# Seventeen products of zeros on TensorE, in the front of a windowed attention with two MoE layers

## The chip, the cores and the metric

The kernel runs on one core of a Trainium2 chip. The metric is the time of one execution on the device in microseconds (us). Before the change three runs took 639.21, 640.41 and 640.44 us; the median is 640.41 us.

## What is computed

Windowed attention with block summaries, then two feed-forward layers on its output, all in float32:

```python
# q, k, v: (2, 8, 768, 64); block 32, window 16, scale 1/8
k_sum = k in blocks of 32, max over the block        # 24 summary keys
v_sum = v in blocks of 32, mean over the block
scores_l = scale * q @ k.T, only where |pos_q - pos_k| < 16
scores_s = scale * q @ k_sum.T + log(32)
a = softmax over [scores_l, scores_s]
x = a @ [v, v_sum]                                   # (1536, 512)
h = relu(x @ w_in);  x = (h * h) @ w_out             # d_ff 2048
xn = x / sqrt(mean(x * x) + 1e-6) * rms_g
out = (silu(xn @ w_gate) * (xn @ w_val)) @ w_out2    # d_ff 1536
```

## The kernel before, in words

The 1536 tokens are 12 groups of 128 (two batches of 6 groups). For a group g the attention has these steps, each a helper of the program:

- `qprep(g)` transposes the queries of groups g and g+1 on TensorE (`qps`, L431) and scales them on ScalarE into `qT` (L433).
- `scores(g)` multiplies queries and keys into two PSUM tiles `s0_g` and `s1_g`. For the first four groups the mask is added by products of an identity with the mask, one ahead (L486) and one behind (L501) the score products (L493).
- `softmax(g)` takes maxima on VectorE (`mx`, L529), exponentials with sums on ScalarE (`t`, `sm`, L535), and normalises on VectorE (L543 to L545). For g < 3 it works in two halves of the heads.
- `ptrans(g)` transposes the probabilities on TensorE (`pps`, L555) and copies them to `pT` on ScalarE (L558).
- `av(g)` multiplies them with the values (`xps1_g`, L578); `split_xs` puts the result into a high part `xhi` on ScalarE (L568) and a low part `xlo` on VectorE (L569).

All weights come as float32 words and are turned into pairs of a high and a low part by a chain of ScalarE steps (L203, L204, L223) and VectorE steps (L210, L211, L214, L217, L224), one chunk at a time: `wi0` to `wi3` and `wo0` to `wo3` in the front. A product of two split matrices is three products of parts (`mm3`). The first feed-forward layer's first chunks (`h_pair`, L617; `y_pair`, L639) are interleaved with the attention of the later groups, so that `h0_0_0` (hidden chunks 0 and 1 of token groups 0 and 1) follows soon after attention group 1. A hidden chunk is squared and split in turn (`r`, L798 and L799; `hhi`, `hlo`, L628 and L629). The rest of the program is products of the two feed-forward layers.

What sets the order: the program text gives the order in which steps are recorded, and a scheduler with a model of the engines lays the instructions out on each engine's own queue; `after(mark)` (`tc.issue_after`) makes it place what is recorded inside it behind the marked instruction. PSUM tiles come from pools with tags: in the front the tags "a" and "x" turn by turn (two banks each), and "h" with two banks.

At the start of the program, TensorE multiplies a tile of zeros `wz` with itself ten times (`WARM`) into a PSUM tile `ws`, and nothing reads the result:

```python
    for _ in range(WARM):
        nc.tensor.matmul(ws, wz, wz, start=True, stop=True)
```

Of the kernel before, what the change touches and what calls it, by code (L numbers as in the profile page):

```python
# [10 lines left out]
F32 = mybir.dt.float32  # L11
# [21 lines left out]
def tile_window_attention_moe_moe2(  # L33
# [13 lines left out]
    nc = tc.nc  # L47
    B, H, S, D = q.shape
    NT, DM = out.shape
    P = 128  # L50
# [38 lines left out]
    psB = ctx.enter_context(tc.tile_pool(name="psB", bufs=1, space=PSUM))  # L89
# [208 lines left out]
    WARM = 10  # L298
# [30 lines left out]
    mark = {}  # L329

    def after(*marks):
        es = ExitStack()
        for m in marks:
            es.enter_context(tc.issue_after(mark[m].ins))
        return es
# [3 lines left out]
    def psA(name, shape=None):  # L339
        tag = rot["tags"][rot["i"] % len(rot["tags"])]  # L340
        rot["i"] += 1
        pool, bufs = {"a": (psB, 2), "h": (psB, 2), "y": (psY, MT // 2), "x": (psX, 2)}[tag]
        return pool.tile(shape or [P, 512], F32, tag=tag, name=name, bufs=bufs)
# [20 lines left out]
    def prep_begin(b):  # L364
        ksum = ap_.tile([P, NPAIR, NB], F32, tag="ksum", name=f"ksum{b}", bufs=1)
        state[b] = ksum
# [54 lines left out]
    def qload(g):  # L421
        b, r = divmod(g, GPB)
        state[("q", g)] = token_chunk(q, b, r // 2, f"qr{g}")

    def qprep(g):
        qr = state.pop(("q", g))
        qT2 = ap_.tile([P, NPAIR, 2 * P], F32, tag="qT", name=f"qT{g}", bufs=QB)
        for j in range(2):
            ps = psA(f"qps{g}_{j}", [P, NPAIR, P])
            for p in range(NPAIR):  # L430
                nc.tensor.transpose(ps[:, p, :], qr[:, j, p * P : (p + 1) * P], ident)  # L431
            with after(*((("exp", 1),) if g == 2 else ())):
                nc.scalar.mul(qT2[:, :, j * P : (j + 1) * P], ps, scale)  # L433
        state[("qT", g)] = state[("qT", g + 1)] = qT2
# [28 lines left out]
    def vload(g, eng=None):  # L463
        b, r = divmod(g, GPB)
        i0 = 2 * g % NVX

        for u in range(2):
            t0 = r * P + u * QT
            rows = [
                (0, G0, t0 - WIN) if t0 else (WIN, WIN, 0),  # L470
                (K1, QT, t0 + WIN) if t0 + QT < S else (K1, QT - WIN, t0 + WIN),
            ]
            for j, n, o in rows:
                (eng or nc.sync).dma_start(
                    vx[j : j + n, i0 + u], v[b, :, o : o + n, :].rearrange("h s d -> s h d")
                )

    def scores(g):
        b, r = divmod(g, GPB)
        qT = state[("qT", g)][:, :, (r % 2) * P : (r % 2 + 1) * P]  # L480
        sl = [psA(f"s{e}_{g}", [P, NPAIR, NK]) for e in range(2)]
        wide = [P, NPAIR, NK]
        if g < NPE:
            for s_ in sl:
                mh = mhi["mid" if r else "first"]
                nc.tensor.matmul(s_, identr, mh.unsqueeze(1).to_broadcast(wide), start=True, stop=False)  # L486
        for p in range(NPAIR):
            for x in range(2):
                for e in range(2):
                    u = (e + x) % 2  # L490
                    o = STEP * (2 * r + u)
                    rr = slice(QT * e, QT * e + QT)
                    mark[("s", g)] = nc.tensor.matmul(  # L493
                        sl[e][QT * u : QT * u + QT, p, :],
                        qT[rr, p, QT * u : QT * u + QT],
                        kT[rr, p, o : o + NK],
                        start=g >= NPE, stop=g >= NPE,
                    )
        if g < NPE:
            for s_ in sl:  # L500
                mark[("s", g)] = nc.tensor.matmul(  # L501
                    s_, identr, mlo.unsqueeze(1).to_broadcast(wide), start=False, stop=True
                )
        state[("s", g)] = sl
# [56 lines left out]
    def split_xs(ps, g, ph):  # L561
        c, m = divmod(g, MT)
        if (ph, c) not in xs:
            new_xs(c, ph)
        hi, lo = xs[(ph, c)]
        pv = ps.rearrange("d (k s) -> d k s", k=KD)
        hv = hi[:, :, m * P : (m + 1) * P]
        mark[("xhi", g, ph)] = nc.scalar.copy(hv, pv)  # L568
        mark[("xlo", g, ph)] = nc.vector.tensor_tensor(lo[:, :, m * P : (m + 1) * P], pv, hv.bitcast(F32), op=ALU.subtract)  # L569

    def av(g):
        pT = state.pop(("pT", g))
        ps = psA(f"xps1_{g}")
        for u in range(2):
            for p in range(NPAIR):
                o = p * P + QT * u
                for e in range(2):
                    nc.tensor.matmul(  # L578
                        ps[QT * e : QT * e + QT, o : o + QT],
                        vx[:, (2 * g + u) % NVX, 2 * p + e, :],  # L580
                        pT[:, e * NPAIR + p, QT * u : QT * u + QT],
                        start=True, stop=True,
                    )
        split_xs(ps, g, 1)
        state["done"] = g
# [131 lines left out]
    def group(g):  # L717

        scores(g)
        if g > 3:  # L720
            vload(g)
        softmax(g)
        if g + 2 < NG and g % 2 == 0:
            qload(g + 2)
# [3 lines left out]
    wz = cpool.tile([P, P], F32, name="wz")  # L728
    nc.vector.memset(wz, 0.0)
    nc.scalar.activation(ss[:, 0:1], wz[:, 0:1], AF.Exp)  # L730
    ws = psY.tile([P, P], F32, tag="y", name="ws", bufs=MT // 2)
    for _ in range(WARM):
        nc.tensor.matmul(ws, wz, wz, start=True, stop=True)
    prep_begin(0)
    for c in range(NC2):
        prep_load(0, c)
# [30 lines left out]
    ptrans(1)  # L767
    qprep(2)
    av(0)
    group(2)  # L770
    vload(2)
    rot["tags"] = ("y",)
    group(3)
    rot["tags"] = ("a", "x")
    av(1)
    vload(3)
    ptrans(2)
# [18 lines left out]
    def square(ps, nm):  # L796
        t = t2(f"r{nm}")
        nc.scalar.activation(t, ps, AF.Relu)  # L798
        nc.vector.tensor_tensor(t, ps, t, op=ALU.mult)  # L799
        return t  # L800
# [36 lines left out]
    for k_ in range(NK2):  # L837
        g, last = 2 * k_ + 3, 2 * k_ + 3 >= NG
        h_pair(k_, 0)
        if k_ == 0:  # L840
            av(2)
            group(4)
# [70 lines left out]
    for i in range(n1 + 2):  # L913
        if i < n1:
# [7 lines left out]
            t = square(ps, f"{c}_{f}")  # L922
# [236 lines left out]
```

## Time and profile before

| | before |
|---|---|
| median of three runs | 640.41 us |
| time of the profiled execution | 640.82 us |
| its span, first to last instruction | 639.1 us |
| TensorE busy | 626.1 us |
| VectorE busy | 457.4 us |
| ScalarE busy | 366.2 us |
| mean granted TensorE clock | 0.987 |

The profile page is one execution as the hardware profiler saw it. PE is TensorE, DVE is VectorE, ACT is ScalarE, SP is the queue that issues most loads. "Busy" of PE is the union of its instructions, which overlap in the pipeline. The granted clock is the share of full speed that TensorE was given: 1.00 is 2.4 GHz and 0.50 is 1.2 GHz. Times within a profile count from the first instruction. A product of two float32 tiles appears as two records on PE, a transpose as one.

### The profile page before, as it was taken

To read this page: it belongs to the slowest core of one execution; us is meant where nothing else is said; L and a number is where in the kernel's file an instruction comes from. 1 tells how busy PE (TensorE), PEld (TensorE's weight loads), DVE (VectorE), ACT (ScalarE), POOL (GpSimd) and SP (SyncE) were. 2 spreads that over 40 slices of the span, in tenths; PEclk is the share of its full clock that TensorE was granted. 3 is DMA by queue.
4 is the path that set the end of the run, shared out by engine and by line. 5 is a ranking of instruction groups with operands and counts; after the bars stand their busy time and mean duration, and the time that the engine had idled before them with its cause. 6 is when DMAs were issued, how large, how long until landed. Compare 5 with 4: busy or idle time off the path is not lost.

```text
span 639.1 us, 9547 instructions
## 1 busy us (share of the span) xinstructions
PE 626.1 (98%) x3578; PEld 518.3 (81%) x3578; DVE 457.4 (72%) x830; ACT 366.2 (57%) x767; POOL 58.1 (9%) x87
## 2 busy tenths in 40 slices
PE   8889999999999999999999999999999999999997
PEld 6568887888888888888888888888888888888885
DVE  4789766969995289986486889489499399561423
ACT  5687676677673266564553767457367277353241
POOL 5021210000000000000000000003004003022040
PEclk9859999999999999999999999999999999999999
DMA  9999812445232123321020115218428319017063
GB/s 255 309 194 159 193 42 50 114 150 179 84 102 96 34 66 100 99 67 34 0 73 28 34 49 182 67 39 179 112 67 172 94 63 183 15 16 118 1 97 101
DMA packets 84430, 64.19 MB, mean 100 GB/s; under 512 B 50368, under 2 KB 73920, under 8 KB 84384
## 3 DMA queue, kind: packets, MB, share of 16 engines
q1 hardware_dynamic: 72976, 51.32, 27.0%
q0 software_dynamic: 11408, 12.26, 13.5%
q8 instruction: 28, 0.46, 0.3%
q14 instruction: 18, 0.15, 0.1%
HBM read 49.94 MB, written 13.63 MB: 99 GB/s over the span
## 4 chain that ended last, share of the span: by engine, by line
PE 87%; DVE 6%; SPq 3%; ACT 2%; DMA 1%; issue 1%; ACTq 0%; DVEq 0%
PE h L617 19%; PE y L639 19%; PE z L639 15%; PE qa L974 10%; PE v L617 5%; PE g L617 5%; PE qc L974 5%; PE qb L974 3%; PE xps L578 2%; SPq L358 2%; PE s L493 1%; PE pps L555 1%; PE xps L595 1%; ACT t L535 1%; DMA raw_wi<-in_moe_w_in_dram 1%; DVE t L521 1%
## 5 line engine op out<-in xcount | busy, mean ns | idle before, releaser
L617 PE MATMUL h<-xhi,w_wi 128*128 128x512 f32 (+1 forms) x480 | 133.5, 352 | 0.0
L639 PE MATMUL y<-w_wo,hhi 128*128 128x512 f32 x384 | 116.7, 392 | 0.4 <-ACT hhi L628 0.4
L617 PEld LDWEIGHTS h<-xhi,w_wi 128*128 128x128 f32 x480 | 86.1, 192 | 12.0 <-ACT t L535 0.2
L639 PE MATMUL z<-w_wp,hhiz 128*128 128x512 f32 x288 | 85.8, 390 | 0.0
L617 PE MATMUL h<-xlo,w_wi 128*128 128x512 f32 (+1 forms) x240 | 84.0, 351 | 0.0
L639 PEld LDWEIGHTS y<-w_wo,hhi 128*128 128x128 f32 x384 | 71.3, 188 | 15.5 <-ACT hhi L628 0.6
L1009 POOL DMA_DIRECT2D out_dram<-zs x40 | 34.9, 1130 | 497.5 <-ACT zs L1005 495.0
L639 PE MATMUL y<-w_wo,hlo 128*128 128x512 f32 x192 | 72.3, 392 | 0.0
L639 PEld LDWEIGHTS z<-w_wp,hhiz 128*128 128x128 f32 x288 | 53.9, 188 | 11.1
L639 PE MATMUL z<-w_wp,hloz 128*128 128x512 f32 x144 | 53.0, 389 | 0.0
L798 ACT ACTIVATE r<-h 128x512 f32<-128x512 f32 x48 | 28.7, 598 | 40.2 <-PE h L617 40.2
L617 PEld LDWEIGHTS h<-xlo,w_wi 128*128 128x128 f32 x240 | 46.1, 192 | 5.9 <-DVE xlo L569 0.2
L799 DVE TENSOR_TENSOR r<-h,r 128x512 f32<-128x512 f32 x48 | 32.9, 685 | 21.5 <-ACT r L798 21.2
L639 PEld LDWEIGHTS y<-w_wo,hlo 128*128 128x128 f32 x192 | 35.7, 188 | 7.3 <-issue 0.2
L628 ACT CAST hhi<-r 128x512 fp32r<-128x512 f32 x48 | 29.7, 620 | 19.2 <-DVE r L799 18.9
L629 DVE TENSOR_TENSOR hlo<-r,hhi 128x512 fp32r<-128x512 f32 x48 | 32.8, 684 | 8.1 <-ACT hhi L628 7.8
L617 PE MATMUL g<-x,w_wg 128*128 128x512 f32 x144 | 34.6, 389 | 0.0
L617 PE MATMUL v<-x,w_wv 128*128 128x512 f32 x144 | 34.6, 389 | 0.0
L1059 DVE TENSOR_TENSOR v<-qc,v 128x512 f32<-128x512 f32 x12 | 8.3, 692 | 35.4 <-ACT v L1058 35.4
L1005 ACT COPY zs<-z 128x512 f32<-128x512 f32 x48 | 26.8, 592 | 11.9 <-PE z L639 11.0
L639 PEld LDWEIGHTS z<-w_wp,hloz 128*128 128x128 f32 x144 | 27.0, 188 | 5.7
L617 PEld LDWEIGHTS g<-x,w_wg 128*128 128x128 f32 x144 | 27.0, 188 | 5.6
(206 smaller groups left out, 1228.3 us busy)
## 6 DMA issues: line engine op xcount, KB each, us to landing
out_dram<-zs POOLq DMA_DIRECT2D x40, 256.0 KB, 6.2
raw_wi<-in_moe_w_in_dram SPq DMA_DIRECT2D x16, 512.0 KB, 5.0
raw_wo<-in_moe_w_out_dram SPq DMA_DIRECT2D x16, 512.0 KB, 4.5
raw_wg<-in_moe_w_gate_dram SPq DMA_DIRECT2D x12, 512.0 KB, 3.4
raw_wv<-in_moe_w_val_dram SPq DMA_DIRECT2D x12, 512.0 KB, 3.6
raw_wp<-in_moe_w_out_dram SPq DMA_DIRECT2D x12, 512.0 KB, 5.8
kr<-in_k_dram SPq DMA_DIRECT2D x12, 256.0 KB, 4.0
qr<-in_q_dram SPq DMA_DIRECT2D x12, 256.0 KB, 5.3
```

Of the source, the lines that this page charges most:

```text
L358: nc.sync.dma_start(t[:, j].rearrange("p (h d) -> p h d", h=H), src[b, :, o : o + P, :].rearrange("h p d -> p h d"),)
L578: nc.tensor.matmul(ps[QT * e : QT * e + QT, o : o + QT], vx[:, (2 * g + u) % NVX, 2 * p + e, :], pT[:, e * NPAIR + p, QT * u : QT * u + QT ...
L617: pe["last"] = nc.tensor.matmul(ps, a_, b_, start=(i == 0), stop=(i == tot - 1))
L628: nc.scalar.copy(hi[:, 0:n], s[:, 0:n]),
L629: nc.vector.tensor_tensor(lo[:, 0:n], s[:, 0:n], hi[:, 0:n].bitcast(F32), op=ALU.subtract),
L639: pe["last"] = nc.tensor.matmul(y, a_[:, ms], b_, start=(first and i == 0), stop=(last and i == 2))
L798: nc.scalar.activation(t, ps, AF.Relu)
L799: nc.vector.tensor_tensor(t, ps, t, op=ALU.mult)
L974: last = nc.tensor.matmul(ps, w[a_][:, kk], x[b_][:, kk], start=start and n == 0, stop=n == 3 * K2 - 1, skip_group_check=not start,)
L1005: nc.scalar.copy(s, ys.pop(m))
L1009: nc.gpsimd.dma_start(out[g * P : (g + 1) * P, :], s, accum_op=ALU.add)
L1059: nc.vector.tensor_tensor(v1[f], C[f], v1[f], op=ALU.add)
```

## The change

Ten lines of the front. The helper `turn_over` records n products of zeros behind the given marks. It replaces the loop at the start (the same ten products), and is called twice more: seven products behind the last product of `av(0)`, ahead of `scores(2)`, and ten behind the last mask product of `scores(3)`. Both write a new PSUM tile `ws2` of the tag "h", which nothing reads. `av` now leaves a mark on its products.

```diff
@@ av(g)
-                    nc.tensor.matmul(
+                    mark[("av", g)] = nc.tensor.matmul(
...
     ws = psY.tile([P, P], F32, tag="y", name="ws", bufs=MT // 2)
-    for _ in range(WARM):
-        nc.tensor.matmul(ws, wz, wz, start=True, stop=True)
+    def turn_over(t, n, *marks):
+        with after(*marks):
+            for _ in range(n):
+                nc.tensor.matmul(t, wz, wz, start=True, stop=True)
+
+    turn_over(ws, WARM)
...
     av(0)
+    ws = psB.tile([P, P], F32, tag="h", name="ws2", bufs=2)
+    turn_over(ws, 7, ("av", 0))
     group(2)
     vload(2)
     rot["tags"] = ("y",)
     group(3)
+    turn_over(ws, 10, ("s", 3))
     rot["tags"] = ("a", "x")
     av(1)
```

The scheduler also lays out other instructions in another order, from group 2 on. Three places show what the prediction speaks of.

TensorE behind scores 3, from the last mask product to the stream of h0_0_0. In the names `pps2_1` is the second half of the transposes of group 2, `xps1_2` the attention output of group 2. Before:

```order
L501 MATMUL s1_3_456<-mstage_84 128x480
L555 MATMUL pps2_0_517<-ident_78,t2_429 120x128 x4
L431 MATMUL qps4_0_530<-ident_78,qr4_448 128x128 x4
L578 MATMUL xps1_1_493<-pT1_360,vx_93 64x64 x8
L555 MATMUL pps2_1_523<-ident_78,t2_429 120x128 x4
L578 MATMUL xps1_1_493<-pT1_360,vx_93 64x64 x8
L578 MATMUL xps1_2_608<-pT2_516,vx_93 64x64
L493 MATMUL s1_4_628<-kT_92,qT4_529 64x120 x8
L431 MATMUL qps4_1_536<-ident_78,qr4_448 128x128 x4
L578 MATMUL xps1_2_608<-pT2_516,vx_93 64x64 x4
L617 MATMUL h0_0_0_542<-xhi1_0_403,w_wi0_555 128x256
L578 MATMUL xps1_2_608<-pT2_516,vx_93 64x64 x2
```

With the change:

```order
L735 MATMUL ws2_407<-wz_98 128x128 x10
L555 MATMUL pps2_0_535<-ident_78,t2_437 120x128 x4
L431 MATMUL qps4_0_548<-ident_78,qr4_456 128x128 x4
L578 MATMUL xps1_1_511<-pT1_360,vx_93 64x64 x8
L555 MATMUL pps2_1_541<-ident_78,t2_437 120x128 x4
L578 MATMUL xps1_1_511<-pT1_360,vx_93 64x64 x8
L431 MATMUL qps4_1_554<-ident_78,qr4_456 128x128 x4
L578 MATMUL xps1_2_626<-pT2_534,vx_93 64x64 x8
L493 MATMUL s1_4_646<-kT_92,qT4_547 64x120 x5
L617 MATMUL h0_0_0_560<-xhi1_0_403,w_wi0_573 128x256
L493 MATMUL s1_4_646<-kT_92,qT4_547 64x120 x3
L617 MATMUL h0_0_2_700<-xhi1_0_403,w_wi2_701 128x256
```

The ten products of zeros stand between scores 3 and the transposes of group 2. Behind the last row four more products of xps1_2 follow, so that ahead of the stream of h0_0_0 there are now 12 of them instead of 7, and one of h0_0_2.

VectorE at the softmax of group 2, beside the conversion of weight chunk wi2 (`x_wi2`). Before:

```order
L211 TENSOR_SCALAR x_wi2_562<-x_wi2_562 128x512
L529 TENSOR_REDUCE mx2_430<-s0_2_407 128x4
L214 SCALAR_TENSOR_TENSOR x_wi2_562<-raw_wi2_347,x_wi2_562 128x512
L529 TENSOR_REDUCE mx2_430<-s1_2_408 128x4
L217 ISA x_wi2_562<-x_wi2_562,u_wi2_563 128x1024
L543 TENSOR_SCALAR sm2_431<-sm2_431 128x4
L529 TENSOR_REDUCE mx3_478<-s0_3_455 128x4
L544 RECIPROCAL sm2_431<-sm2_431 128x4
L529 TENSOR_REDUCE mx3_478<-s1_3_456 128x4
L545 TENSOR_TENSOR t2_429<-t2_429,sm2_431 128x480
```

With the change:

```order
L211 TENSOR_SCALAR x_wi2_580<-x_wi2_580 128x512
L214 SCALAR_TENSOR_TENSOR x_wi2_580<-raw_wi2_347,x_wi2_580 128x512
L217 ISA x_wi2_580<-x_wi2_580,u_wi2_581 128x1024
L529 TENSOR_REDUCE mx2_438<-s0_2_415 128x4
L529 TENSOR_REDUCE mx2_438<-s1_2_416 128x4
L224 TENSOR_TENSOR w_wi2_701<-x_wi2_580,w_wi2_701 128x512
L543 TENSOR_SCALAR sm2_439<-sm2_439 128x4
L544 RECIPROCAL sm2_439<-sm2_439 128x4
L529 TENSOR_REDUCE mx3_486<-s0_3_463 128x4
L545 TENSOR_TENSOR t2_437<-t2_437,sm2_439 128x480
```

The merge (L214) and the add (L217) of wi2 moved ahead of both maxima of group 2, and one maximum of group 3 moved behind the first normalisation. On ScalarE the rounding copy of wi2 (L223) moved from behind the exponentials of group 2 to ahead of them.

ScalarE at the cast of `hhi0_1_0`, behind the last product of y0_0 (its copy is `yp1`), with the change:

```order
L652 COPY yp1_945<-y0_0_1_824 128x512
L805 ACTIVATE r0_1_0_1007<-h0_1_0_982 128x512
L393 COPY kT_92<-kps1_1_1_910 128x2x4x16
L394 COPY kT_92<-kps1_1_1_910 128x2x4x48
L393 COPY kT_92<-kps1_2_0_927 128x2x4x16
L394 COPY kT_92<-kps1_2_0_927 128x2x4x48
L568 CAST xhi1_1_965<-xps1_4_948 128x4x128
L393 COPY kT_92<-kps1_2_1_935 128x2x4x16
L394 COPY kT_92<-kps1_2_1_935 128x2x4x48
L433 ACTIVATE qT6_969<-qps6_0_970 128x4x128
L628 CAST hhi0_1_0_1010<-r0_1_0_1007 128x512
```

Before, the cast stood ahead of all copies of keys (`kT`) of batch 1, three places behind the relu `r0_1_0`; now it stands behind them and behind the copies of xps1_4 and qps6_0.

## Rows read from the trace of the kernel before

**Rows 1.** The page, busy us of each engine, share of the span, instructions.

```profile
PE 626.1 (98%) x3578; PEld 518.3 (81%) x3578; DVE 457.4 (72%) x830; ACT 366.2 (57%) x767; POOL 58.1 (9%) x87
```

**Rows 2.** Windows by stage: us, busy of each engine (instructions), clock, DMA.

```profile
36.00:50.00 14.00, 14.00 (x115) 11.87 (x115) 10.91 (x23) 10.81 (x28) 3.50 (x3) 0.55 1.04 187
50.00:70.00 20.00, 20.00 (x199) 17.99 (x196) 17.91 (x32) 11.64 (x32) 3.92 (x3) 1.00 1.01 163
...
140.00:600.00 460.00, 460.00 (x2102) 382.05 (x2101) 336.16 (x617) 256.46 (x455) 27.99 (x32) 1.00 0.32 82
```

**Rows 3.** Windows of one us; the number behind POOL's is the granted clock.

```profile
28.00:29.00 1.00, 1.00 (x21) 0.91 (x24) 0.38 (x1) 0.58 (x2) 0.00 (x0) 0.52 1.03 418
...
31.00:32.00 1.00, 1.00 (x33) 1.00 (x32) 1.00 (x3) 0.06 (x1) 0.00 (x0) 0.77 1.02 401
...
34.00:35.00 1.00, 0.00 (x0) 0.00 (x0) 1.00 (x4) 1.00 (x7) 0.00 (x0) 0.94 1.10 249
35.00:36.00 1.00, 0.42 (x2) 0.45 (x3) 1.00 (x3) 1.00 (x6) 0.51 (x1) 0.50 0.44 105
...
48.00:49.00 1.00, 1.00 (x8) 1.00 (x8) 0.89 (x3) 1.00 (x3) 0.09 (x1) 0.74 1.09 247
```

**Rows 4.** Timeline of TensorE: start us, us, what, records [idle before].

```profile
1.14 3.92 PE L733 MATMUL ws<-wz 128*128 128x128 f32 x20 [1.14 <-DVE wz L729]
...
4.34 0.72 PE L733 MATMUL ws<-wz 128*128 128x128 f32 x5
...
11.83 1.05 PE L493 MATMUL s<-kT,qT 64*64 64x120 f32 x32
...
13.45 1.05 PE L493 MATMUL s<-kT,qT 64*64 64x120 f32 x32
...
27.46 0.70 PE L486 MATMUL s<-mstage 128*128 128x480 f32 x2 [1.66 <-ACT pT L558]
28.10 1.88 PE L493 MATMUL s<-kT,qT 64*64 64x120 f32 x32
...
32.18 0.70 PE L501 MATMUL s<-mstage 128*128 128x480 f32 x2
35.58 1.08 PE L555 MATMUL pps<-ident,t 128*120 128x128 f32 x4 [2.70 <-DVE sm L543]
...
38.50 1.11 PE L555 MATMUL pps<-ident,t 128*120 128x128 f32 x4
...
45.20 0.58 PE L617 MATMUL h<-xlo,w_wi 128*128 128x256 f32 x1
...
49.59 0.80 PE L578 MATMUL xps<-pT,vx 120*64 120x64 f32 x18
```

**Rows 5.** The products of zeros at L733: duration ns min/median/max.

```profile
L733 PE MATMUL ws<-wz x20: 275/421/582, 1.1 to 4.8; 128*128 128x128 f32 x20
```

**Rows 6.** Timeline of VectorE: conversion of wi1 and wi2, first maximum of group 2.

```profile
26.40 0.43 DVE L211 TENSOR_SCALAR x_wi<-x_wi 128x512 uint32<-128x512 uint32 x1
26.86 0.69 DVE L214 SCALAR_TENSOR_TENSOR x_wi<-raw_wi,x_wi 128x512 uint32<-128x512 uint32 x1
27.69 0.69 DVE L217 CUSTOM_DVE_ANT_0 x_wi<-x_wi,u_wi 128x1024 uint16<-128x1024 uint16 x1
...
30.85 0.43 DVE L211 TENSOR_SCALAR x_wi<-x_wi 128x512 uint32<-128x512 uint32 x1
31.19 0.65 DVE L529 TENSOR_REDUCE mx<-s 128x4 f32<-128x480 f32 x1
```

**Rows 7.** Timeline of ScalarE: the first exponential of group 2.

```profile
31.94 0.36 ACT L535 ACTIVATE t<-s,mx 128x120 f32<-128x120 f32 x1 [1.28 <-DVE mx L529]
```

**Rows 8.** Timelines of TensorE and ScalarE near 76 us.

```profile
76.29 1.15 PE L578 MATMUL xps<-pT,vx 120*64 120x64 f32 x32
77.37 1.09 PE L431 MATMUL qps<-ident,qr 128*128 128x128 f32 x8
78.06 1.09 ACT L433 ACTIVATE qT<-qps 128x512 f32<-128x512 f32 x2
```

## The prediction, made before the changed kernel ran

> **What bounds the kernel now.** I read the engines' totals first, then the windows by stage, then the windows of one microsecond with the granted clock, then the timelines of TensorE (PE), VectorE (DVE) and ScalarE (ACT) around the two places of the change. TensorE is busy 626.1 of 639.1 us [rows 1], and from 140 to 600 us it is never idle [rows 2]. So a microsecond that TensorE gains in the front stays gained, unless another engine takes it back. Waste is in the front: from 36 to 50 us TensorE is busy all the time, yet at a mean granted clock of 0.55 [rows 2].
>
> The windows of one microsecond show where the clock was lost [rows 3]. It fell at about 28 us, came back near 31.5 us, fell again near 34.9 us and came back near 48.5 us; in between it stood at 0.50, that is 1.2 instead of 2.4 GHz. What the engine did before each fall stands in its timeline [rows 4]. Before the first it had idled 1.66 us, between the products of attention group 0 and the mask of scores 2, until a copy on ACT freed a PSUM bank. The second fall came inside an idle of 2.70 us behind scores 3, which ended when DVE had normalised the first half of group 2. The change fills these two idles with products of zeros.
>
> **What it removes, adds and moves.** *Seven products ahead of scores 2.* One product of zeros is two records. At the full clock five records took 0.72 us, and the last lasts 0.275 us, so a record takes (0.72 - 0.275)/4 = 0.11 us and a product 0.22 us [rows 4, 5]. Seven take 1.56 us and fit the idle of 1.66 us; the mask behind them waits for ACT, which does not change. Cost: 0. If the clock were at 1.2 GHz, they would take twice that, 3.1 us, and push scores 2 back by about 1.4 us. Do zeros hold the clock? The first thing TensorE runs is 10 such products [rows 4]: the longest record is 582 ns and the shortest 275 ns [rows 5], so it sped up while running nothing else. I take it that the first fall goes.
>
> *Scores 2 and 3 at full clock.* They ran from 28.10 to about 32.83 us, partly at 0.50. Scores 0 took from 11.83 to 13.45 us, 1.62 us at the full clock [rows 4], so the two end near 28.10 + 2 x 1.62 = 31.3 us, 1.5 us earlier. What waits for them is DVE's first maximum of group 2. In the program before, DVE took it at 31.19 us, right after the second shift of weight chunk wi2 at 30.85 us [rows 6]. In the changed order two more steps of that weight chunk, the merge (L214) and the add (L217), stand ahead of it, and on ACT the rounding copy of wi2 stands ahead of the exponentials. So the 1.5 us are worth nothing here, and the softmax gets later. For chunk wi1 the same chain took 26.86 - 26.40 = 0.46 us from shift to merge and 27.69 - 26.86 = 0.83 us to the add [rows 6]. From 30.85 that gives the add at 32.14 us, ending at 32.83; the maximum starts 0.6 us behind it, near 32.75, and ends at 33.4. ACT's exponentials, which began at 31.94, 0.10 us after their maximum [rows 6, 7], begin at 33.5 us: 1.55 us later. Before, 35.58 - 31.94 = 3.64 us lay between them and the transposes of group 2 [rows 4, 7]; that gives 37.1. But of the two maxima of group 3 that DVE took in between, one now stands behind. A maximum is 0.65 us long [rows 6], some 0.4 of which count here, since DVE's instructions overlap a little and the reciprocal now waits for the step before it. So the transposes start at 36.7 us instead of 35.58. Bounds: the old 35.58, if DVE has room that I do not see, and 37.1.
>
> *Ten products behind scores 3.* From 31.3 us, 10 x 0.22 = 2.2 us, so they end at 33.6 us. Nothing waits for them: cost 0 (at 1.2 GHz 4.4 us from 32.8, past 36.7 by 0.5 us). But they leave 36.7 - 33.6 = 3.1 us of idle, longer than the 1.66 us and the 2.70 us before which the clock fell. So in the likeliest case the clock still falls, only later, while the transposes of group 2 and the first products of attention group 1 run. These cost 2.92 us at 1.2 GHz (35.58 to 38.50 [rows 4]) and about 1.6 us at 2.4; the second half of the transposes waits for DVE anyway, near 38.3 us instead of 38.50. So up to there the change gains 0.2 us. From there on TensorE has the same work as before at 1.2 GHz, until the long stream of products for the first hidden chunk (L617), which began at 45.20 us, brings the clock back near 48.5 us [rows 3, 4]. The new order puts 5 more products of attention group 2 and one of h0_0_2 ahead of that stream. They are done at the slow clock and not again later, and cost about 0.5 us more there; with the 0.2 us the sum is +0.3 us at worst and, if the clock comes back a little earlier in the stream's work, -0.2 us. I take 0.
>
> *The rest of the front, in another order.* The program is laid out by a scheduler, and the 17 products shift its choices as far as the second MoE round. The clearest place is near 76 us. ACT's cast of hhi0_1_0 now stands behind eight copies that start when the last product of y0_0 is done. A copy takes 0.5 us [rows 8], so the cast is done after about 4.0 us, while TensorE has only 3.3 us of other work (4 transposes of keys, 16 products of attention 4 in 1.1 us, 8 transposes of queries in 1.1 us [rows 8] and as many of group 5). That is a stall of 0.7 us, between 0 (if ACT is ahead) and 1. I take 0.4, since the sum lets ACT begin with nothing done. The DMAs are the same ones; four loads of values move ahead of the key chunks on SP, which are used far behind: 0.
>
> **Sum.** 0 (seven products) + 0 (scores) + 0 (ten products and what follows) + 0.4 (order) = +0.4 us against the profiled execution's 640.82 (span 639.1 and 1.7 around it), 641.2. That execution stands 0.4 us above the median of 640.41, so against the median I say 640.8. A measurement of this kernel can tell about 0.2%, 1.3 us, from no change, so this is no change.
>
> The page "TensorE: Matmul & The Clock Gate" of the Trainium skill (part on the transpose mode) says that transposes through TensorE do not count as busy for the clock in the way that products do. By it the work that follows the second idle, which begins with eight transposes, could not hold the clock, and the time would be the forecast's or the first rival's. The trace shows transposes with products among them at a clock of 0.50 from 35.6 us on without a rise, which agrees, but no stretch of transposes alone.
>
> **Rivals.** *The clock is given back later (slower).* The place is the L617 stream. Its unbroken part starts near 46.1 us in my sum instead of 45.2 (0.9 us: five products and one more at 1.2 GHz, with the changes between them), or near 47 if the clock falls before the transposes of group 2 are taken up. Before, the clock came back in the midst of that stream. If it now stays at 0.50 for one more stretch as long as the one from 28.05 to 31.46, 3.4 us of work take twice their time: +1.7 us. With the 0.4 us of the order the time is 640.4 + 2.1 = 642.5. It decides when the return comes later than about 50 us. For it: softmax 2 gets later by the order on DVE and ACT. Against it: 0.9 us is a small shift. Chance 0.25.
>
> *The clock holds to the end of the front (faster).* If 3.1 us of idle are not enough, after so many products of zeros, TensorE has after 38.3 us half the time to spend: from 38.50 to 49.59 us, the end of the first hidden chunk [rows 4], it spent 11.1 us, 10 of them at 0.50. It then waits for ACT's copies of group 2 and is at the stream near 42.3 us, 2.9 us earlier, and done with it some 4.5 us earlier. DVE, which is busy 17.9 of 20 us from 50 to 70 us [rows 2], takes back about 1.5 us, and the order 0.4: -2.6 us, 637.8. For it: of the stretch in which the clock fell the second time, 2.2 us are now filled. Against it: both falls came with less idle than the 3.1 us that stay. Chance 0.30.
>
> *The zeros do not hold the clock at all.* Then the second ten run at 1.2 GHz, end at 39.3 us and push the transposes of group 2 back by 2.6 us: 643. Rows 5 speak against it; 0.03.
>
> The same page says (part on the clock gate) that the moments at which the clock changes are not tied to the kernel's start and differ between runs. By it the first two rivals and the forecast could all be seen in runs of the same kernel, and the median would be the forecast's. The times of before lie between 639.21 and 640.44, which neither shows nor excludes it.
>
> **How the numbers follow.** The forecast has 0.42, the later return 0.25, the held clock 0.30, zeros without effect 0.03. The forecast's own range takes the bounds of its terms, -0.2 + 0 and +0.3 + 1: 640.2 to 641.7. With the held clock and the later return the range goes from 637.4 (0.4 us below, for what DVE takes back) to 642.6. Faster by over 0.2% comes from the held clock and little else: 0.33. Slower comes from the later return, less those cases in which it costs under 1.3 us, and from the zeros without effect: 0.25. Within 0.2%: 0.42.
>
> **What would show it.** Right: no fall near 28 us; scores 3 done near 31.3; DVE's first maximum of group 2 near 32.75 and the transposes behind the ten products at 36.7; a clock of 0.50 from some point between 35.6 and 38.3 us to about 48.5 or later; a wait for hhi near 76 us. Wrong: transposes of group 2 at 35.6 us or earlier, which would make the rest of my chain wrong; a clock of 1.00 throughout; TensorE waits above 1 us between 50 and 140 us that I have not named.

## The result, and the profile after

The changed kernel took 649.93 us (median of 6 runs, 648.23 to 651.81), the kernel before beside it 640.58 (6 runs, 639.21 to 643.09). The ratio is 1.0143, 95% interval [1.0126, 1.0159]: 9.3 us slower, outside the predicted range of 637.4 to 642.6 us. The profiled execution took 649.32 us, its span is 647.6.

The page of the changed kernel, busy us of each engine [rows 1 for before]:

```profile
PE 627.3 (97%) x3612; PEld 519.9 (80%) x3612; DVE 458.3 (71%) x830; ACT 364.7 (56%) x767; POOL 57.7 (9%) x87
```

TensorE is busy only 1.2 us longer, zeros included, yet the span grew by 8.5. So most of the loss is idle time; in the busy time a gain of clock in the front, the added zeros and a loss of clock behind the front nearly cancel. Where they lie is read from the windows by stage (us, busy of each engine with instructions, granted clock, DMA share, GB/s). After:

```profile
36.00:50.00 14.00, 10.55 (x137) 8.93 (x137) 11.95 (x26) 12.44 (x44) 4.00 (x3) 1.00 0.94 165
...
70.00:90.00 20.00, 19.42 (x181) 16.47 (x184) 9.99 (x16) 10.96 (x25) 2.45 (x2) 1.00 0.56 132
90.00:110.00 20.00, 17.25 (x214) 13.25 (x204) 12.82 (x20) 11.79 (x46) 2.02 (x2) 0.91 0.10 22
110.00:130.00 20.00, 16.95 (x214) 14.89 (x210) 18.61 (x32) 12.30 (x31) 0.00 (x0) 1.00 0.33 87
130.00:140.00 10.00, 7.93 (x62) 6.70 (x63) 7.63 (x14) 9.71 (x39) 0.00 (x0) 0.83 0.86 278
140.00:600.00 460.00, 460.00 (x2152) 382.94 (x2151) 340.20 (x624) 259.69 (x463) 27.98 (x32) 1.00 0.32 82
```

The four of these stages that [rows 2] do not show, before:

```profile
70.00:90.00 20.00, 19.96 (x226) 16.58 (x225) 14.64 (x24) 14.04 (x43) 4.80 (x4) 1.00 0.53 129
90.00:110.00 20.00, 19.29 (x227) 16.54 (x227) 13.73 (x21) 14.67 (x49) 0.00 (x0) 1.00 0.18 41
110.00:130.00 20.00, 19.55 (x226) 17.55 (x226) 18.01 (x33) 14.74 (x38) 0.00 (x0) 1.00 0.45 134
130.00:140.00 10.00, 9.68 (x84) 8.01 (x83) 7.53 (x13) 8.52 (x27) 0.00 (x0) 1.00 0.43 152
```

Two things changed places. From 36 to 50 us the clock is 1.00 instead of 0.55 [rows 2], as the zeros were meant to bring about. From 70 to 140 us TensorE idles 8.45 us (0.58 + 2.75 + 3.05 + 2.07) instead of 1.52, and the clock falls twice where it never fell before: 0.91 of 20 us and 0.83 of 10 us are 1.8 and 1.7 us of lost work. The windows of one microsecond show that each fall came about 1 us after the end of a wait, at 102 and at 133 us:

```profile
101.00:102.00 1.00, 1.00 (x10) 1.00 (x11) 0.00 (x0) 1.00 (x7) 0.00 (x0) 1.00 0.00 0
102.00:103.00 1.00, 1.00 (x8) 1.00 (x7) 0.53 (x3) 1.00 (x4) 0.00 (x0) 0.58 0.00 0
...
132.00:133.00 1.00, 0.93 (x4) 0.67 (x4) 0.95 (x2) 1.00 (x4) 0.00 (x0) 0.94 1.10 400
133.00:134.00 1.00, 1.00 (x12) 0.56 (x12) 0.97 (x3) 1.00 (x6) 0.00 (x0) 0.50 1.08 422
```

The timeline of TensorE (start, us, what, records [idle before <- what ended it]) names the waits. After:

```profile
56.97 1.20 PE L639 MATMUL y<-w_wo,hhi 128*128 128x512 f32 x4
...
88.67 1.09 PE L639 MATMUL y<-w_wo,hhi 128*128 128x512 f32 x4
89.69 1.05 PE L493 MATMUL s<-kT,qT 64*64 64x120 f32 x32
...
100.97 1.06 PE L555 MATMUL pps<-ident,t 128*120 128x128 f32 x8 [2.31 <-DVE t L545]
...
112.81 0.50 PE L617 MATMUL h<-xhi,w_wi 128*128 128x256 f32 x2 [1.61 <-ACT xhi L568]
114.36 0.38 PE L617 MATMUL h<-xlo,w_wi 128*128 128x256 f32 x1 [1.05 <-DVE xlo L569]
...
132.07 1.44 PE L639 MATMUL y<-w_wo,hhi 128*128 128x512 f32 x4 [2.46 <-ACT hhi L628]
```

The same stretch, and where y0_0 starts, before:

```profile
58.39 0.98 PE L639 MATMUL y<-w_wo,hhi 128*128 128x512 f32 x3
...
82.30 1.05 PE L493 MATMUL s<-kT,qT 64*64 64x120 f32 x32
...
85.33 1.51 PE L493 MATMUL s<-kT,qT 64*64 64x120 f32 x32
86.77 0.50 PE L617 MATMUL h<-xhi,w_wi 128*128 128x256 f32 x2
...
92.93 1.03 PE L555 MATMUL pps<-ident,t 128*120 128x128 f32 x8
```

Before, scores 6 and 7 (82.30 and 85.33) stood ahead of the 48 products of h0_2 (from 86.77), which hid the softmax of group 6; its transposes followed at 92.93 without a wait. In the changed order h0_2 and four products of y0_2 go first, and scores 6 start at 89.69 (7.4 us later). The rest of y0_2 is used up before softmax 6 is done, so its transposes wait 2.31 us.

Softmax 6 itself also takes longer now. Counted from the start of scores 6 to the end of its normalisation, it took 89.92 + 1.16 - 82.30 = 8.8 us before and takes 99.66 + 1.16 - 89.69 = 11.1 us after. VectorE shows what stands in between. Before, the maximum of group 6 is taken ahead of the masking of scores 7, and no copy stands ahead of the normalisation:

```profile
84.66 1.15 DVE L533 TENSOR_REDUCE mx<-t 128x8 f32<-128x960 f32 x1
...
87.17 1.21 DVE L521 TENSOR_TENSOR t<-s,mask_mid 128x480 f32<-128x480 f32 x2
...
89.92 1.16 DVE L545 TENSOR_TENSOR t<-t,sm 128x960 f32<-128x960 f32 x1
```

After, the masking of group 6 starts behind the low part of a chunk of h0_2 (90.93). Half of the masking of scores 7 and a copy of value means (92.79) stand ahead of the maximum, which starts at 94.08. A copy of y0_2 stands ahead of the normalisation:

```profile
93.50 0.66 DVE L521 TENSOR_TENSOR t<-s,mask_mid 128x480 f32<-128x480 f32 x1
...
98.63 0.68 DVE L652 COPY yp<-y 128x512 f32<-128x512 f32 x1
...
99.66 1.16 DVE L545 TENSOR_TENSOR t<-t,sm 128x960 f32<-128x960 f32 x1
```

TensorE's work from scores 6 to their transposes shrank from 10.6 to 9.0 us, which would still have covered 8.8 us; it does not cover 11.1. Both are read from the traces; no run separates the order on TensorE from that on VectorE.

Behind this wait the next ones follow: h0_3 waits for the split of group 7 (1.61 + 1.05 us), y0_3 for the cast of its hidden chunk (2.46). These are waits above 1 us that the prediction had not named, its sign of being wrong.

The balance of the two executions: y0_0 starts at 56.97 instead of 58.39, 1.4 us ahead. Behind it come 6.9 us more of idle and 3.5 us of lost clock: -1.4 + 6.9 + 3.5 = +9.0, where the spans differ by 8.5.

### The profile page after: what moved, and what is told of

Read it like the earlier page. It is cut to its first block, busy times and chain, and to the rows that moved or that the text cites. A ratio compares the mean times of both kernels' runs of the same rounds, so it can differ in the third digit from the quotient of the medians.

```text
span 647.6 us, 9612 instructions
## 1 busy us (share of the span) xinstructions
PE 627.3 (97%) x3612; PEld 519.9 (80%) x3612; DVE 458.3 (71%) x830; ACT 364.7 (56%) x767; POOL 57.7 (9%) x87
## 4 chain that ended last, share of the span: by engine, by line
PE 85%; DVE 6%; SPq 3%; ACT 2%; DMA 2%; issue 1%; DVEq 0%; ACTq 0%
PE y L639 19%; PE h L617 19%; PE z L639 15%; PE qa L981 10%; PE g L617 5%; PE qc L981 5%; PE v L617 5%; PE qb L981 3%; PE xps L578 2%; SPq L358 1%; SPq L474 1%; DMA raw_wi<-in_moe_w_in_dram 1%; PE s L493 1%; ACT t L535 1%; PE xps L595 1%; DMA raw_wo<-in_moe_w_out_dram 1%
## 5 line engine op out<-in xcount | busy, mean ns | idle before, releaser
L617 PE MATMUL h<-xhi,w_wi 128*128 128x512 f32 (+1 forms) x480 | 131.8, 349 | 1.6 <-ACT xhi L568 1.6
L617 PEld LDWEIGHTS h<-xhi,w_wi 128*128 128x128 f32 x480 | 84.7, 189 | 13.8 <-ACT xhi L568 1.8
L617 PEld LDWEIGHTS v<-x,w_wv 128*128 128x128 f32 x144 | 27.0, 188 | 5.6
```

The costliest lines, as they stand in the source:

```text
L617: pe["last"] = nc.tensor.matmul(ps, a_, b_, start=(i == 0), stop=(i == tot - 1))
```

## The experiments

The first four take the order and the zeros apart by small edits. Each ratio is to the kernel before, run beside it.

**scores_ahead.** All zeros stay; h0_2 is put behind scores 7.

```diff
-        h_pair(k_, 0)
+        with after(*((("s", 7),) if k_ == 2 else ())):
+            h_pair(k_, 0)
```

> All seventeen products of zeros stay; the first hidden chunk of token groups 4 and 5 (h0_2) is put behind scores 7 on TensorE, so that scores 6 and 7 stand ahead of it as before the change. Theory (the new order of scores 6 and 7 costs the time): the loss goes, 637.5 to 641 us; TensorE idles less than 3 us in all between 60 and 150 us, and its clock does not fall there. Rival (the zeros themselves, or what they shift in the front up to 57 us): 647 us or more, with idle and clock falls as in the changed kernel.

Measured: 643.87 us, 1.0032 [1.0017, 1.0047]. The windows have no clock fall behind 90 us, and 3.4 instead of 7.9 us of idle:

```profile
90.00:110.00 20.00, 18.25 (x226) 15.15 (x226) 13.79 (x22) 14.73 (x50) 0.00 (x0) 1.00 0.18 41
110.00:130.00 20.00, 18.39 (x217) 16.14 (x213) 18.84 (x34) 14.53 (x37) 0.00 (x0) 1.00 0.45 131
130.00:140.00 10.00, 10.00 (x85) 8.26 (x84) 6.53 (x11) 8.26 (x26) 0.00 (x0) 1.00 0.46 160
```

This one edit gives back 1.1% of the 1.4%, some 7 us. But the time stays 2.8 us above the median of before and above the theory's range: something else in the new order costs, or the zeros do.

**scores_late_no_zeros.** The kernel before; every product of scores 6 and 7 gets an edge behind the last product of h0_2.

```diff
+        if k_ == 2:
+            for i in mark[("sl", 6)] + mark[("sl", 7)]:
+                tc.add_manual_dep(i.ins, pe["last"].ins.name, ...)
```

> The kernel before, without the seventeen products, but with scores 6 and 7 put behind h0_2 on TensorE. From there on every engine's order is that of the changed kernel. Theory (order): 648 to 652 us, with some 2 us of idle ahead of the transposes of group 6, 2.5 ahead of h0_3 and 2.5 ahead of y0_3, and one or two clock falls between 95 and 140 us. Rival (the zeros): 642 us or less.

Measured: 651.55 us, 1.0165 [1.0127, 1.0203]. The waits of TensorE (us in total, times, longest) are those of the changed kernel, without one added product:

```profile
PE pps L556 <- DVE sm L544: 2.7, 1, 2.7
PE y L640 <- ACT hhi L629: 2.6, 1, 2.6
PE h L618 <- ACT xhi L569: 2.3, 2, 1.6
PE s L486 <- ACT pT L559: 2.2, 1, 2.2
PE pps L556 <- DVE t L546: 1.7, 1, 1.7
PE h L618 <- DVE xlo L570: 1.6, 3, 1.0
```

The 2.7 and the 2.2 are the two idles of the front [rows 4]; the others are the new ones. So moving scores 6 and 7, with what the scheduler then moves behind them on the other engines, is enough for the whole loss.

**seven_only** leaves out the call with ten products. The order of every engine is then exactly that of the changed kernel.

> The seven products ahead of scores 2 alone; every engine's order is otherwise exactly that of the changed kernel. Theory (order): as slow as the changed kernel, 649 to 653 us, the upper end if the clock falls behind scores 3 as before the change (up to 2.9 us more). Rival (each product of zeros costs): about 7/17 of the loss, 643 to 646 us.

Measured: 651.51 us, 1.0169 [1.0136, 1.0203], as the theory has it.

**ten_only** leaves out the call with seven.

> The ten products behind scores 3 alone. The scheduler then leaves scores 6 and the first half of scores 7 ahead of h0_2, though other steps move too. Theory (order): no loss, 638 to 642 us; the clock falls near 28 us as before the change. Rival (each product of zeros costs): 10/17 of the loss, 645 us or more.

Measured: 644.39 us, 1.0061 [1.0041, 1.0081]. Neither end: scores 6 are ahead of h0_2, and more than half of the loss is gone, but this is a third order with other waits (y0_0 waits 2.08 us for a cast of hhi at 61.65). Runs in which the scheduler chooses again do not isolate the zeros.

The next four therefore hold the order. A table lists each engine's first rows (TensorE 1300, ScalarE 300, VectorE 310, SP 110; behind them the orders of before and after are the same), and each row gets an edge to the one ahead. In the traces TensorE, VectorE and ScalarE then run in that order throughout. Line numbers are some 60 higher in these kernels.

```diff
+ORDER = {
...
+def lay_out(nc, tc, skip):
...
+        for a, b in zip(row, row[1:]):
+            tc.add_manual_dep(b, a.name, info, reason="order")
```

**zeros_order_before**: the seventeen products in the order of before.

> All seventeen products, with every engine's order held as it was before the change by a written table; only the products of zeros are added to TensorE's row. Theory (order costs, zeros gain a little): the clock does not fall at 28 us and holds longer behind 35 us, transposes of group 2 start 8.1 us behind the start of scores 2 as before, and y0_0 starts 28 us or so behind it instead of 30.9; 637.5 to 640.5 us beside 641. Rival 1 (the 2.8 us by which the run with scores 6 ahead stays above the kernel before come from the zeros): 643 to 645 us. Rival 2 (VectorE and ScalarE set the pace behind 57 us and take all of it back): 640.5 to 642 us.

Measured: 640.50 us, 0.9995 [0.9976, 1.0013]: no difference that shows. The time is where the theory's range ends and that of rival 2 begins, so the trace has to decide. The windows:

```profile
36.00:50.00 14.00, 13.33 (x162) 11.73 (x163) 11.98 (x26) 12.31 (x35) 3.81 (x3) 1.00 1.04 181
50.00:70.00 20.00, 18.11 (x164) 15.74 (x163) 19.28 (x32) 12.14 (x33) 3.94 (x3) 1.00 0.97 160
```

The clock is 1.00 in all its windows, and y0_0 starts at 54.98 instead of 58.39. But from 50 to 70 us TensorE now idles 1.9 us, where before it had none [rows 2], 1.4 of it for VectorE and 0.5 for ScalarE, while VectorE is busy 19.28 of 20. By scores 6 (80.49 instead of 82.30) 1.8 us are left, and at 134 us another wait for VectorE (1.48) takes 1.2 of them. In this execution rival 2 of the expectation holds: VectorE takes most of the held clock back.

**order_after_no_zeros**: no added product, in the order of the changed kernel.

> No added product of zeros, and every engine's order held as it is in the changed kernel. Theory (order): 650 to 653 us, that is what seven products alone gave (651.5) or up to 1.5 us more or less by the clock. Rival (the zeros are part of the loss): 646 us or less.

Measured: 651.67 us, 1.0177 [1.0145, 1.0209]. With it the four corners are there:

| order of the engines | without zeros | with seventeen |
|---|---|---|
| as before | 640.68 us | 640.50 us, ratio 0.9995 |
| as in the changed kernel | 651.67 us, ratio 1.0177 | 649.93 us, ratio 1.0143 |

The order is worth 1.5 to 1.8%. The zeros are worth nothing that shows in the old order, and in the new one 0.3% less time, which is not resolved, since the intervals overlap.

**seven_order_before** and **ten_order_before** split the zeros in the old order.

> The seven products alone, every engine's order as before. Theory: the clock still falls behind scores 3, the time lies between that of the kernel before and that of all seventeen, 639 to 641.5 us. Rival 1 (zeros cost): 642 us or more.

> The ten products alone, every engine's order as before. Theory: the clock falls near 28 us and comes back near 31.5, so the ten run at full clock and fill 2.2 of the 2.7 us behind scores 3; 638 to 641 us. If the ten meet a low clock they take 4.4 us and push the transposes of group 2 back by 1.7: 641 to 643. Rival 1 (zeros cost): 643 us or more.

Measured: 641.91 us, 1.0015 [0.9997, 1.0034], and 640.38 us, 0.9991 [0.9976, 1.0006]. Neither part can be told from no change, although the seven alone lie above the range of their theory. The clock went as expected: with seven alone it falls behind scores 3 (0.78 from 36 to 50 us), with ten alone near 28 us (0.79 from 28 to 36) and not behind them.

**softmax2_late** looks for the 2.8 us that scores_ahead left: old order, all zeros, and only the piece of wi2 from the changed order, which the prediction had worked out.

> All seventeen products and every engine's order as before, except one piece that is taken from the changed kernel: on VectorE the merge and the add of weight chunk wi2 stand ahead of the maxima of group 2, and on ScalarE the rounding copy of wi2 ahead of the exponentials of group 2. The transposes of group 2 should start some 9 us behind the start of scores 2 instead of 8.1. Theory (VectorE sets the pace behind 50 us, so this piece is hidden, as the prediction had it): 640 to 641.5 us. Rival (this piece is what keeps the run with scores 6 ahead at 643.9): 643 to 644.5 us.

Measured: 642.56 us, 1.0020 [1.0002, 1.0038], between the two theories and some 0.25% above zeros_order_before. Its timeline of TensorE and the window behind:

```profile
31.98 2.39 PE L799 MATMUL ws<-wz 128*128 128x128 f32 x20
37.36 1.08 PE L617 MATMUL pps<-ident,t 128*120 128x128 f32 x4 [2.99 <-DVE t L607]
```

```profile
36.00:50.00 14.00, 12.64 (x93) 10.68 (x94) 10.86 (x24) 11.20 (x37) 4.17 (x3) 0.52 1.02 182
```

The ten products end, 2.99 us of idle remain, and the clock is down, with a mean of 0.52 up to 50 us. In this execution the prediction's likeliest case is seen step for step, up to the return, which is late as in its first rival (642.5 us). But it is one of the slowest of the twelve (643.61 us), and its mean clock of 0.988 is the lowest. Seven of the twelve had 0.997 or more, and their median is still 642.05 us, where the ten executions of zeros_order_before with 0.997 or more have 640.09 (the kernel before beside them: 641.14 and 640.68). So the fall of the clock is not what sets the median apart. By the ratios the piece costs some 1.6 us, and where these go in the usual execution was not seen. The rest of the 2.8 stays with smaller moves (scores_ahead waits 1.28 us ahead of the transposes of group 6, inside h0_2); it was not taken apart further.

**early_softmax2** follows from what the zeros cover up. The idle ahead of scores 2 is a queue order on ScalarE: the copy that frees the bank stands behind the conversion of wi1, which waits for its load. Before:

```profile
25.23 0.68 ACT L203 ACTIVATE x_wi<-raw_wi 128x512 f32<-128x512 f32 x1 [1.71 <-DMA raw_wi<-in_moe_w_in_dram]
...
26.85 0.57 ACT L558 COPY pT<-pps 120x512 f32<-120x512 f32 x1
```

The table is edited there, in VectorE's softmax 2 and in TensorE's h0_0_0; ten products stay. **early_no_zeros** is the same without them.

> The ten products, and the order as before but for three pieces of the table: on ScalarE the copies that free the banks for scores 2 stand ahead of the conversion of wi1, which waits for its load; on VectorE the softmax of group 2 stands ahead of most of wi1 and wi2; on TensorE h0_0_0 stands ahead of the transposes of queries 4. Theory (the idle ahead of scores 2 is a queue order on ScalarE, and is worth more removed than filled): scores 2 start near 26 us without a wait, y0_0 starts near 54 us or earlier, 636.5 to 639.5 us. Rival (VectorE sets the pace up to 67 us whatever comes before): 640 to 641.5 us.

> The same order without any added product of zeros. Theory (the zeros are worth the clock behind scores 3 and little of the time): the clock falls behind scores 3, and the time is within 1.5 us of the run with ten products. Rival (a held clock is worth 2 us or more once VectorE is relieved): 2 to 4 us above that run.

Measured: 639.93 us, 0.9979 [0.9965, 0.9992], and 640.41 us, 0.9987 [0.9972, 1.0003]. On ScalarE the copies of the run with ten products now come first, and the conversion waits by itself:

```profile
24.82 0.59 ACT L619 COPY pT<-pps 120x512 f32<-120x512 f32 x1
...
27.85 0.66 ACT L264 ACTIVATE x_wi<-raw_wi 128x512 f32<-128x512 f32 x1 [0.62 <-DMA raw_wi<-in_moe_w_in_dram]
```

Scores 2 start at 26.53 without a wait and the transposes of group 2 at 32.53, some 3 us earlier than in any run above. Only 0.2% comes of it, a time between those of the theory and of the rival. In the profiled execution TensorE then waits for VectorE, and the clock falls behind that wait: from 50 to 70 us 0.83 of 20 us are 3.4 us of lost work, and y0_0 starts at 56.91, not near 54 or earlier as in the theory:

```profile
PE s L554 <- DVE xlo L630: 2.4, 1, 2.4
```

```profile
50.00:70.00 20.00, 18.75 (x149) 16.56 (x150) 17.84 (x30) 10.87 (x31) 3.94 (x3) 0.83 1.04 173
```

With ten products the interval lies below 1, so this version is faster than the kernel before, by little. Without them it reaches 1.0003, and it overlaps that of zeros_order_before. So it is not shown that an idle moved out by order is worth more than one that is filled. The ten products are worth 0.08% here, which the intervals do not resolve either.

**early_softmax4** moves that xlo and its neighbours ahead of the conversions of wo0 and wo1.

> As the run with the early softmax 2 and ten products, and one piece more of the table: on ScalarE the relu of h0_0_0, the copy of xps1_2 and the copies of group 3 stand ahead of the conversions of wo0 and wo1, and on VectorE their partners (r0_0_0, xlo1_0 of group 2, the mask and maximum of group 4) too, since TensorE waited 2.42 us at 51.25 us for that xlo. Theory (that wait is a queue order on VectorE): the wait falls below 0.5 us, y0_0 starts near 54.5 us, 638 to 639.7 us. Rival (VectorE has the same sum of work up to 67 us, and hands the wait on to y0_0 or to the transposes of group 5): y0_0 or pps4 and pps5 wait 1.5 us or more instead, 639.5 to 641 us.

Measured: 640.55 us, 0.9985 [0.9973, 0.9998]. The time lies in the rival's range, not the theory's. The wait for xlo is gone and y0_0 starts at 51.56, as the theory had it. But a wait as long turns up behind its first products, for ScalarE and not, as the rival had it, ahead of y0_0 or of transposes for VectorE:

```profile
57.19 0.50 PE L678 MATMUL h<-xhi,w_wi 128*128 128x256 f32 x2 [2.40 <-ACT xhi L629]
```

## Why the prediction was wrong, step by step

**Seven products: right.** They start at 27.09, and TensorE then waits 0.34 us for the same copy on ScalarE; the clock does not fall near 28 us (1.00 from 28 to 36 us, 0.72 before). Its reading of the first ten products is weaker than it sounds: their records get shorter, but the granted clock of before is 1.00 in every window from 1 to 5 us, so no rise of the clock is seen there.

**Scores and softmax 2: the times are right once the start is moved; that they cost nothing is not.** In this execution the load of wi1 landed later, and VectorE's second shift of wi2 stands at 32.60 instead of 30.85 [rows 6]: 1.75 us that the change did not make (scores 2 start at 28.2 to 29.6 us in every other run whose front keeps the order of before or of the changed kernel; the profiled execution of before, with 27.46 [rows 4], was the early one, and with its front ten_order_before and seven_order_before stand at 29.25 and 29.27). VectorE and, below it, ScalarE, after:

```profile
32.60 0.43 DVE L211 TENSOR_SCALAR x_wi<-x_wi 128x512 uint32<-128x512 uint32 x1
...
34.49 1.22 DVE L529 TENSOR_REDUCE mx<-s 128x4 f32<-128x480 f32 x2
```

```profile
35.24 0.36 ACT L535 ACTIVATE t<-s,mx 128x120 f32<-128x120 f32 x1
```

Less 1.75 us the maximum stands at 32.74 (said: 32.75) and the exponentials at 33.49 (33.5). TensorE:

```profile
33.02 2.39 PE L735 MATMUL ws<-wz 128*128 128x128 f32 x20
38.39 0.62 PE L555 MATMUL pps<-ident,t 128*120 128x128 f32 x4 [2.97 <-DVE t L545]
```

The transposes are at 36.64 (36.7), the ten products took 2.39 us (2.2), and 2.97 us of idle remain (3.1). The chain was read rightly, step for step. The price of 0 for the later softmax, though, is not borne out: softmax2_late stands 0.25% above zeros_order_before.

**The clock behind them: the rival with chance 0.30 in this execution, the forecast's case in that of softmax2_late.** Here it held, and y0_0 came 3.2 us earlier when both are counted from scores 2 (27.72 instead of 30.93 us), between the 2.9 and the 4.5 of that rival. But the other engines take back nearly all, not 1.5 us: zeros_order_before measures -0.05% (0.3 us), where the rival said -2.6 us with 0.4 for the order in it.

**The rest of the front, in another order: the step that failed.** It was priced at +0.4 us with bounds 0 and 1, from one place, the cast of hhi0_1_0 near 76 us. The size was about right there, the cause not: TensorE waited 0.20 and 0.38 us, for copies of keys, and not for that cast. The term was mis-sized by what the same reordering did 10 us later. Scores 6 and 7 moved behind h0_2, which measures +1.65% without any zeros (scores_late_no_zeros), 10.6 us, more than ten times the upper bound. The order of the instructions was there to be read. What was left out is to follow it at the next pair of scores and transposes, with two questions: which filler stands between them now, and which steps stand inside the softmax now? From the start of scores 6 to the transposes it takes 100.97 - 89.69 = 11.3 us after, 2.31 of them idle, and took 92.93 - 82.30 = 10.6 us before without a gap. The filler alone would not have told: 9.0 us of it are left, and the softmax had taken 8.8. The wait comes of both, since softmax 6 now takes 11.1 us with the steps of scores 7 and of y0_2 ahead of its own on VectorE.

**Sum and range.** Zeros alone, in the old order, change nothing that shows (0.9995), so the first three terms add up to about 0 there; with the later softmax of group 2 they come to some 1.3 us (softmax2_late, 1.0020). The fourth carries the error, and with it the range. No rival had the order as its mechanism. A slip of the prediction stands beside this: in the rival of zeros without effect its own terms put the end of the second ten products at 32.83 + 1.4 + 4.4 = 38.6 us, not at 39.3. The forecast does not use it.

## What to carry to other kernels

Where a scheduler lays out the program, an added instruction has two prices, its own and that of the order that comes of it; take them apart by holding the order. Price the second at every place where a wait is hidden by other work, not at the clearest one alone, and ask both what still hides it and what has moved into the chain that is hidden. An idle that is filled hides its cause: find what the releasing instruction was queued behind. A lead on the busiest engine is kept only as far as the next engine has room, here VectorE, busy 19.28 of 20 us from 50 to 70.

## What the runs showed of the hardware

The same idle does not always cost the clock. Behind the ten products 2.97 to 2.99 us of idle remained in three executions: the mean granted clock from 36 to 50 us was 1.00 in the changed kernel, 0.88 in scores_ahead, whose front has the same order, and 0.52 in softmax2_late. Without zeros and with the front of before, scores_late_no_zeros shows 0.76 there, before 0.55 [rows 2]. The page "TensorE: Matmul & The Clock Gate" of the Trainium skill (part on the clock gate) says that the moments of the change are not tied to the kernel's start and differ between runs of one kernel. The two pairs with one front (1.00 and 0.88, 0.76 and 0.55) agree.

The mean granted clock of every execution is on record, and the time goes with it. Of 93 executions of the kernel before beside the runs, 25 had a clock of 0.987 or less and took 642.01 to 643.84 us (median 642.69); 54 had 0.994 or more, with a median of 640.45. By its clock of 0.987 the profiled execution of before is one of the 25 (it took only 640.82, with scores 2 early). So the 0.55 from 36 to 50 us that the change was to win back was not the usual case. All twelve executions of early_softmax2 had 0.994 or more and took 639.07 to 641.02 us. That the clock alone makes these differences was not shown.
